# Between two stages of a fused attention and Fourier-mixing kernel: roots and foldings swapped, transposes pinned, copies and memsets moved to another engine

## The chip, the cores and the metric

The kernel runs on one core of a Trainium2 chip. The metric is the device time of one execution in microseconds, as a median over executions. Engines are named as in the profile: PE is TensorE (PEld its weight loads), DVE is VectorE, ACT is ScalarE, POOL is GpSimd, SP is the engine that starts most of the DMAs.

## What is computed

The reference has two parts, one after the other. The first is attention with "talking heads": 8 batches, 12 heads, 448 positions, 64 columns per head. The scores of all heads are mixed by a 12 x 12 matrix before the softmax, and the probabilities are mixed by another one after it. The second is an FNet block on the result, seen as 448 x 768 per batch: the real part of a two-dimensional Fourier transform is added, the rows are normalised, and a feed-forward layer of width 3072 follows. In short:

```python
scores = scale * np.matmul(q, k.transpose(0, 1, 3, 2))
scores = np.einsum('bhij,hg->bgij', scores, w_pre)
attn = softmax(scores)
attn = np.einsum('bhij,hg->bgij', attn, w_post)
x = join_heads(attn @ v)
u = x + np.real(fft2(x))
un = (u - mean(u)) / np.sqrt(var(u) + 1e-06)
out = u + np.maximum(un @ w_ch1, 0.0) @ w_ch2
```

The two weight matrices of the feed-forward layer come as 64-bit floats, and the kernel converts them itself, on DVE, in small pieces dealt out between its other work.

## The kernel before

**Two stages.** `mix_phase` does the attention and the Fourier part. It runs over 192 steps (`TOT`, 24 for each batch, `GS`), with an offset for work that is issued ahead, and up to step 197. A step T takes a slab of mixed scores: the products q k (L443) into `Sb`, a DMA regrouping (L459) into `Kr`, the first mixing (L469), the maximum (L477 on DVE), the exponential (L485 on ACT), the reciprocal (L493 and L494 on DVE), the scaling (L496 on POOL), the second mixing (L506), and a transpose on DVE into `Pv` (L517). Six steps make a group, four groups a batch. For each group, three products with v follow (`emit_av`, L533, 56 matmuls each for pr = 0, 1, 2), whose results ACT copies into `XT` (L324). Columns of `XT` that no row fills are set to zero by POOL (L555). Then PE transposes `XT` into `X` (`emit_x`, L566, six transposes in two halves of three).

**Foldings.** The Fourier transform uses symmetry: after every second group of a batch, `fold` puts eight short POOL steps into the list `folds` (sums and differences of rows and columns: L587, L592, L601, L602), and after the fourth group four more (L608), which make `xf`. The loop takes at most two steps from the list in each of its own steps. For the last batch the first eight are listed at step 188 and so are taken in steps 189 to 192; the last twelve are listed in step 197, after the loop's last look at the list, and are issued by `fold_rest`. From `xf` PE makes `z` (`emit_z`, L631) and from `z` the transform (`emit_s2`, L647), which DVE adds to `X` (L658, L660) and which is then stored to DRAM. The last batch's share of this is carried over as `parts` into the second stage and issued between its products.

**The second stage.** `ffn_phase` works on 7 tiles of 512 rows (`NTB`) and 6 column blocks of weights (`NC`). It uses a seven-product scheme for each pair of blocks: `first` (L946) and `second` (L1002), each in the order `ORDER = (0, 4, 5, 1, 6, 2, 3)`. Before the first product, tile 0 needs: `stats` (L892 and L893 on DVE, four rows of tiles x = 0 to 3), `power` (the roots: L897 to L900 on POOL, which make one over the standard deviation), `norm` (L908 on ACT, `un`, two buffers), `turn` (six transposes per x in two halves y of three, L917 on PE into `psQ`, two buffers; a copy of each half into `ub`, L919 on ACT), `total` (four differences, L925 on DVE, and behind the last seven stores to DRAM, L929 on SP), and `load_w2` (seven loads of weights of the second product, L877 on SP). `un` of x = 2 and 3 needs the buffers of x = 0 and 1. Tiles 1 to 6 are normalised between the products of the tile before them.

**What sets the order.** Inside a `manual_schedule` block, the engines that it names keep the order in which the code issues their instructions. Work of other engines, and how two such blocks lie against one another, is placed by a planner, which reckons when each instruction's inputs will be there and takes the earlier one in the code where several are ready. The mixing loop names PE, DVE, ACT and POOL; the statistics and roots name PE, DVE and POOL; the rest of the second stage names PE and DVE. So ACT's order in the second stage, and SP's throughout, are the planner's.

```python
with tc.manual_schedule(engines={ET.PE, ET.DVE, ET.Pool}):
    for x in range(NT2):
        stats(0, x)
    power(0)
    fold_rest()
with tc.manual_schedule(engines={ET.PE, ET.DVE}):
    for x in range(NT2):
        norm(0, x)
        turn(0, x)
    for n in range(4):
        total(0, n)
    for i in ORDER:
        load_w2(0, i)
```

Of the kernel before, what the change touches and what calls it, by code (L numbers as in the profile page):

```python
# [16 lines left out]
P = 128  # L17
# [30 lines left out]
TOT = B * GS  # L48
# [5 lines left out]
MG = 4  # L54
# [39 lines left out]
NK = DM // 2 // P  # L94
# [190 lines left out]
def mix_phase(ctx, tc, rest, ident, q, k, v, w_pre, w_post, u_scr, u_rev, wts):  # L285
# [6 lines left out]
    nc = tc.nc  # L292
# [28 lines left out]
    pend, folds, later = [], [], []  # L321
# [200 lines left out]
    def emit_av(g, pr):  # L522

        st = batches[g["b"]]
        Pv = g["Pv"]
        rp = _row(Pv)
        nu = GT * 4
        pss = [ms_tile() for _ in range(2)]
        for jb in range(C7):
            for x in range(2):  # L530
                for y in range(2):
                    i = 2 * pr + x
                    nc.tensor.matmul(  # L533
                        pss[y][64 * x:64 * x + 64, :nu * R],
                        st["v", pr][64 * y:64 * y + 64, x, jb * D:(jb + 1) * D],
                        _ap(Pv, 64 * y * rp + 32 * jb + R * i,
                            [[rp, 64], [HS, nu], [1, R]]),
                        start=(jb == 0), stop=(jb == C7 - 1))
        if pr == 0:
            g["XT"] = pxt.tile([P, 6, XW], F32, name="XT", tag="XT")  # L540
        XT = g["XT"]
        rx = _row(XT)
        first, sg, none = PLACE[g["gi"]]

        def done(y):
            rs = _row(pss[y])
            for e in range(2):

                o = MG + first + sg * NB * e
                dst = _ap(XT, (3 * y + pr) * XW + o, [[rx, P], [sg * RS, R], [sg, RS]])  # L550
                src = _ap(pss[y], 60 * e, [[rs, P], [1, R], [R, RS]])
                copy(ENG["AV"][y], dst, src)
            if y == 1 and pr == 2:
                for o in none:
                    nc.gpsimd.memset(XT[:, :, MG + o:MG + o + 1], 0.0)  # L555
        return [lambda y=y: done(y) for y in range(2)]

    def emit_x(g):
# [190 lines left out]
    with tc.manual_schedule(engines={ET.PE, ET.DVE, ET.Activation, ET.Pool}):  # L749
        while s <= TOT - GS + AT_X[-1]:  # L750
            old = len(later)
            n = take("none", s)
            if 0 <= s + LM < TOT:
                emit_premix(s + LM)
            flush()
            if 0 <= s < TOT:
                emit_postmix(s)
            if 0 <= s + LM < TOT:
                emit_max(s + LM)
                emit_exp(s + LM)  # L760
            take("AV", s)
            if 0 <= s < TOT:
                emit_turn(s)
            if s >= 4:
                wts.deal(1)
            take("QK", s)
            if 0 <= s + LG < TOT:
                if any(e[2] is not None and e[2] <= (s + LG) // BS for e in pend):
                    flush()
                emit_gather(s + LG)  # L770
            if 0 <= s + LM < TOT:
                emit_scale(s + LM)
            for _ in range(old):
                later.pop(0)()
            for _ in range(min(len(folds), 1 if n and s > 3 else 2)):
                folds.pop(0)()
            take("full", s)
            s += 1
        flush()
        wts.deal(1000)  # L780
# [26 lines left out]
ORDER = (0, 4, 5, 1, 6, 2, 3)  # L807
# [5 lines left out]
def ffn_phase(ctx, tc, rest, ident, u_scr, u_rev, wts, ub_scr, out, fold_rest,  # L813
# [61 lines left out]
    def load_w2(c, i):  # L875
        w2[i] = pw2.tile([P, FM, DH], F32, name="w2t", tag="w2t")
        nc.sync.dma_start(out=w2[i][:, :, :], in_=wts.w2[c][i])  # L877
# [33 lines left out]
    def turn(t, x):  # L911
        un = uns.pop(x)
        for y in range(2):
            ps = ps_tile("Q")
            for c in range(NK):
                cc = NK * y + c
                nc.tensor.transpose(ps[:, c * P:(c + 1) * P],  # L917
                                    un[:, cc * P:(cc + 1) * P], ident[:, :])
            nc.scalar.copy(  # L919
                out=ubs[t, UB[y, x // 2]][:, :, (x % 2) * P:(x % 2 + 1) * P],  # L920
                in_=ps[:, :NK * P].rearrange("p (c n) -> p c n", n=P))

    def total(t, n):
        o, a, b = ((4, 6, 0), (5, 2, 4), (6, 2, 6), (3, 1, 5))[n]
# [112 lines left out]
    with tc.manual_schedule(engines={ET.PE, ET.DVE}):  # L1037
        for x in range(NT2):
            norm(0, x)
            turn(0, x)  # L1040
        for n in range(4):
            total(0, n)
        for i in ORDER:
            load_w2(0, i)
        for n in range(NC * NTB):
            c, t = divmod(n, NTB)

            if c + 1 < NC and 0 <= t - (c == 0) < NK + FM:
                wts.add(c + 1, t - (c == 0))
            wts.deal(0)  # L1050
            if c == 0 and t + 2 < NTB:
                load_u(t + 2)
            second(n, first(n))
            wts.deal(1000)
            if n == 0:
                assert not parts
                rest.close()
                pu.append(pool("pu2", side="right"))
                beside.close()
                pps.append(pool("ppy", space=bass.MemoryType.PSUM))  # L1060
# [61 lines left out]
```

## Time and profile before

| what | value |
|---|---|
| median of 4 executions | 2429.3 us (2423.35 to 2432.78) |
| the profiled execution's own time | 2425.4 us |
| its span, first to last instruction | 2423.6 us |
| mean granted TensorE clock | 0.996 |
| TensorE busy in the stretch 820.0 to 843.6 us | 21.88 of 23.6 us |
| in 843.6 to 853.1 | 0.00 of 9.5 us |
| in 853.1 to 863.2 | 9.75 of 10.1 us |
| in 863.2 to 868.2 | 3.15 of 5.0 us |
| in 1100 to 2424 | 1319.1 of 1324 us |

A span is the time from the first to the last instruction of one profiled execution; its own time contains a little more around it. The seam between the two stages lies at about 840 to 868 us. Busy times of different engines overlap, so they are not to be added up. In a line of the timeline stand the start in us, the duration of the merged group, the engine, the line of the code, the operation, what it writes and reads, how many instructions there are, and in brackets how long the engine was idle before it and what ended that.

### The profile page before, as it was taken

To read this page: it belongs to the slowest core of one execution; us is meant where nothing else is said; L and a number is where in the kernel's file an instruction comes from. 1 tells how busy PE (TensorE), PEld (TensorE's weight loads), DVE (VectorE), ACT (ScalarE), POOL (GpSimd) and SP (SyncE) were. 2 spreads that over 40 slices of the span, in tenths; PEclk is the share of its full clock that TensorE was granted. 3 is DMA by queue.
4 is the path that set the end of the run, shared out by engine and by line. 5 is a ranking of instruction groups with operands and counts; after the bars stand their busy time and mean duration, and the time that the engine had idled before them with its cause. 6 is when DMAs were issued, how large, how long until landed. Compare 5 with 4: busy or idle time off the path is not lost.

```text
span 2423.6 us, 48510 instructions
## 1 busy us (share of the span) xinstructions
PE 2379.7 (98%) x18608; PEld 1552.7 (64%) x18608; DVE 1505.6 (62%) x3103; ACT 798.7 (33%) x2059; POOL 780.6 (32%) x1293
## 2 busy tenths in 40 slices
PE   7999999999999889999999999999999999999999
PEld 2445454544554477777777777777777777777776
DVE  3777778788787747785567356635665457533333
ACT  4777667666666542322101111111111110110110
POOL 3687877868675531221111011101110011000000
PEclk9999999999999999999999999999999999999999
DMA  6555554646554466346444444535443644353331
GB/s 146 177 182 161 178 174 153 199 156 192 166 167 147 157 208 211 128 151 231 148 136 154 143 145 136 156 116 172 142 152 98 199 127 146 121 167 114 118 117 52
DMA packets 168596, 372.10 MB, mean 154 GB/s; under 512 B 36750, under 2 KB 90022, under 8 KB 168366
## 3 DMA queue, kind: packets, MB, share of 16 engines
q1 hardware_dynamic: 129038, 260.22, 33.2%
q0 software_dynamic: 33760, 107.40, 15.3%
q8 instruction: 149, 2.44, 0.4%
q10 hardware_dynamic: 5568, 1.38, 0.3%
q14 instruction: 81, 0.66, 0.1%
HBM read 211.98 MB, written 74.34 MB: 118 GB/s over the span
## 4 chain that ended last, share of the span: by engine, by line
PE 95%; DMA 2%; SPq 1%; DVE 1%; ACT 1%; issue 0%; ACTq 0%; DVEq 0%
PE psP L946 18%; PE psP L1002 18%; PE psR L946 9%; PE psR L1002 9%; PE mx L469 7%; PE po L506 7%; PE ms L443 6%; PE ms L533 6%; PE psQ L1002 5%; PE psQ L946 4%; PE ms L647 2%; PE ms L420 2%; PE ms L631 1%; DMA Kr<-Sb 1%; PE ms L566 1%; PE psQ L917 1%
## 5 line engine op out<-in xcount | busy, mean ns | idle before, releaser
L946 PE MATMUL psP<-ub,w1t 128*128 128x256 f32 x2016 | 462.6, 379 | 0.0
L1002 PE MATMUL psP<-w2t,h 128*128 128x384 f32 x1344 | 461.0, 486 | 0.0
L946 PEld LDWEIGHTS psP<-ub,w1t 128*128 128x128 f32 x2016 | 382.9, 190 | 60.6
L207 POOL DMA_DIRECT2D raw<-in_moe_w_ch_dram x120 | 68.9, 574 | 923.9 <-DVE tmp L251 905.7
L1002 PEld LDWEIGHTS psP<-w2t,h 128*128 128x128 f32 x1344 | 254.5, 190 | 165.8
L496 POOL TENSOR_SCALAR PP<-PP,rcp 128x448 f32<-128x448 f32 x384 | 240.6, 635 | 236.9 <-DVE rcp L494 106.7
L477 DVE TENSOR_REDUCE nmx<-mx 128x1 f32<-128x448 f32 x384 | 222.2, 618 | 128.4 <-PE mx L469 125.8
L485 ACT ACTIVATE PP<-mx,nmx 128x448 f32<-128x448 f32 x384 | 240.1, 630 | 170.6 <-DVE nmx L477 161.8
L951 ACT COPY h<-psP 128x512 f32<-128x512 f32 x42 | 24.6, 585 | 764.4 <-PE psP L946 753.2
L1008 DVE TENSOR_TENSOR u<-u,psP 128x384 f32<-128x384 f32 x336 | 183.5, 552 | 141.3 <-PE psP L1002 139.1
L946 PE MATMUL psR<-ub,w1t 128*128 128x256 f32 x1008 | 231.3, 379 | 0.0
L1002 PE MATMUL psR<-w2t,h 128*128 128x384 f32 x672 | 230.5, 486 | 0.0
L469 PE MATMUL mx<-Kr,kw 60*64 60x448 f32 x1536 | 222.3, 553 | 7.0 <-DMA Kr<-Sb 4.7
L517 DVE STREAM_TRANSPOSE Pv<-po 128x896 f32<-128x896 f32 x192 | 212.8, 1108 | 14.9 <-PE po L506 12.3
L957 DVE TENSOR_TENSOR h<-h,psQ 128x512 f32<-128x512 f32 x42 | 28.9, 687 | 298.8 <-PE psQ L946 298.6
L946 PEld LDWEIGHTS psR<-ub,w1t 128*128 128x128 f32 x1008 | 191.4, 190 | 25.9
L506 PE MATMUL po<-PP,kw 60*32 60x448 f32 x3072 | 189.0, 548 | 1.3 <-DVE rcp L493 1.3
L324 ACT COPY Sb<-ms 124x448 f32<-124x448 f32 x384 | 184.6, 539 | 16.5 <-PE ms L443 7.2
L443 PE MATMUL ms<-kT,qT 64*64 64x448 f32 (+1 forms) x1536 | 189.2, 553 | 0.0
L533 PEld LDWEIGHTS ms<-Pv,vv 64*64 64x64 f32 x5376 | 144.0, 133 | 69.9 <-issue 32.1
L1002 PEld LDWEIGHTS psR<-w2t,h 128*128 128x128 f32 x672 | 127.3, 190 | 87.4
L533 PE MATMUL ms<-Pv,vv 64*64 64x120 f32 x5376 | 167.0, 269 | 0.8 <-issue 0.8
(92 smaller groups left out, 2751.3 us busy)
## 6 DMA issues: line engine op xcount, KB each, us to landing
ub<-ub SPq DMA_DIRECT2D x294, 384.0 KB
Kr<-Sb SPq DMA_DIRECT2D x768, 105.0 KB
raw<-in_moe_w_ch_dram POOLq DMA_DIRECT2D x72, 256.0 KB, 3.5
raw<-in_moe_w_ch_dram POOLq DMA_DIRECT2D x48, 384.0 KB, 3.8
w<-wst POOLq DMA_DIRECT2D x126, 128.0 KB, 3.1
w<-wst POOLq DMA_DIRECT2D x84, 192.0 KB, 3.2
w1t<-w SPq DMA_DIRECT2D x42, 384.0 KB
w2t<-w SPq DMA_DIRECT2D x42, 384.0 KB
```

What stands on the lines that cost most here:

```text
L324: (nc.scalar.copy if eng == "a" else nc.vector.tensor_copy)(out=out, in_=in_)
L443: nc.tensor.matmul(pss[x][64 * y:64 * y + r0 + 64 - lo, :S], st["qT", xx][64 * x:64 * x + 64, y, lo:r0 + 64], st["kT", xx][64 * x:64 * x + ...
L469: nc.tensor.matmul(mx[x][64 * z:64 * z + 64, :S], kw1[64 * x:64 * x + KR, :], Kr[64 * x:64 * x + KR, z, :], start=True, stop=True)
L477: nc.vector.tensor_reduce(nmx[x][:, :], steps[T]["mx"][x][:, :S], axis=AX.X, op=ALU.max, negate=True)
L485: nc.scalar.activation(PP[:, x, :], steps[T]["mx"][x][:, :S], ACTF.Exp, bias=steps[T]["nmx"][x][:, :], accum_out=den[:, x:x + 1])
L496: nc.gpsimd.tensor_scalar(PP[:, x, :], PP[:, x, :], rcp[:, x:x + 1], 1.0, op0=ALU.mult, op1=ALU.mult)
L506: nc.tensor.matmul(po[o:o + 32, z, :S], kw2[64 * z:64 * z + KR, y, :], PP[64 * z:64 * z + KR, :, c * HS:(c + 1) * HS], start=True, stop=True)
L517: nc.vector.transpose(g["Pv"][:, T % GT, :].rearrange("p (z s) -> p z s", z=2), steps[T]["po"][:, :, :S])
L533: nc.tensor.matmul(pss[y][64 * x:64 * x + 64, :nu * R], st["v", pr][64 * y:64 * y + 64, x, jb * D:(jb + 1) * D], _ap(Pv, 64 * y * rp + 32 ...
L946: nc.tensor.matmul(p[:, m, :], w1[i][:, kc, m * P:(m + 1) * P], ub[:, kc, :], start=i in OPENS and m == kc == 0, stop=kc == NK - 1, skip_g ...
L1002: nc.tensor.matmul(p, lhs[i][:, kf, x * P:(x + 1) * P], w2[i][:, kf, :], start=i in OPENS and kf == 0, stop=kf == FM - 1, skip_group_check ...
L1008: nc.vector.tensor_tensor(us_, us_, p, op=ALU.add)
```

## The change

The change makes five edits, all but the first of them at the seam:

1. The memsets of `XT` (32 in all) are issued on DVE instead of POOL.
2. From step `TOT - 3` (189) on the mixing loop takes nothing from the list of foldings. What is left in the list is issued by `fold_rest`, which stands behind `power(0)`.
3. The very first transpose of `turn` (tile 0, x = 0, y = 0, c = 0) is tied to stay behind the PE instruction issued just before it in the code, which is the last transpose of the mixing loop. The tie is one of order in the queue.
4. For tile 0, the copies of the second half of each x (y = 1) are made by DVE, those of the first half by ACT as before.
5. The loads of the second product's first weights are issued before the differences and the stores behind them, not after.

```diff
@@ emit_av @@
             if y == 1 and pr == 2:
                 for o in none:
-                    nc.gpsimd.memset(XT[:, :, MG + o:MG + o + 1], 0.0)
+                    nc.vector.memset(XT[:, :, MG + o:MG + o + 1], 0.0)
@@ mix_phase, the loop @@
-            for _ in range(min(len(folds), 1 if n and s > 3 else 2)):
-                folds.pop(0)()
+
+            if s < TOT - 3:
+                for _ in range(min(len(folds), 1 if n and s > 3 else 2)):
+                    folds.pop(0)()
@@ turn @@
-                nc.tensor.transpose(ps[:, c * P:(c + 1) * P],
-                                    un[:, cc * P:(cc + 1) * P], ident[:, :])
-            nc.scalar.copy(
-                out=ubs[t, UB[y, x // 2]][:, :, (x % 2) * P:(x % 2 + 1) * P],
-                in_=ps[:, :NK * P].rearrange("p (c n) -> p c n", n=P))
+                tr = nc.tensor.transpose(ps[:, c * P:(c + 1) * P],
+                                         un[:, cc * P:(cc + 1) * P], ident[:, :])
+                if t == x == y == c == 0:
+
+                    tc.keep_in_program_order(tr)
+
+            copy = nc.vector.tensor_copy if t == 0 and y else nc.scalar.copy
+            copy(out=ubs[t, UB[y, x // 2]][:, :, (x % 2) * P:(x % 2 + 1) * P],
+                 in_=ps[:, :NK * P].rearrange("p (c n) -> p c n", n=P))
@@ ffn_phase @@
             norm(0, x)
             turn(0, x)
+        for i in ORDER:
+            load_w2(0, i)
         for n in range(4):
             total(0, n)
-        for i in ORDER:
-            load_w2(0, i)
```

## The prediction

> **What bounds the kernel now.** I read the page first, then the waits of TensorE, then the order of time around the one long wait, engine by engine.
>
> ```profile
> PE 2379.7 (98%) x18608; PEld 1552.7 (64%) x18608; DVE 1505.6 (62%) x3103; ACT 798.7 (33%) x2059; POOL 780.6 (32%) x1293
> ...
> PE psQ L917 <- ACT un L908: 10.3, 2, 9.5
> PE ms L420 <- DMA rawq<-in_q_dram: 7.2, 3, 6.2
> PE ms L420 <- DMA rawk<-in_k_dram: 6.0, 1, 6.0
> PE mx L469 <- DMA Kr<-Sb: 4.7, 5, 1.6
> ```
>
> TensorE is busy for 2379.7 of 2423.6 us, so about 44 us is all that any reordering can win, and the longest single wait is 9.5 us: the first transposes of the feed-forward stage (L917) waiting for the first normalised rows (L908). The timeline of each engine around it:
>
> ```profile
> 838.61 1.25 POOL L496 TENSOR_SCALAR PP<-PP,rcp 128x448 f32<-128x448 f32 x2 [3.79 <-DVE rcp L494]
> 840.02 1.03 POOL L670 DMA_INDIRECT v<-X,rows  x1 [0.16 <-issue]
> 841.07 1.97 POOL L587 TENSOR_TENSOR xs<-X 113x384 f32<-113x384 f32 x2
> ...
> 849.71 0.18 POOL L602 COPY xq<-xs 113x1 f32<-113x1 f32 x1
> 849.99 0.25 POOL L897 TENSOR_SCALAR mv<-mv 128x4 f32<-128x4 f32 x1
> ...
> 842.40 0.21 DVE L893 BATCH_NORM_AGGREGATE mv<-st 128x2 f32<-128x12 f32 x1
> ...
> 841.48 0.80 ACT L324 COPY XT<-ms 128x60 f32<-128x60 f32 x4 [3.57 <-PE po L506]
> 852.02 1.95 ACT L908 ACTIVATE un<-u,mv 128x768 f32<-128x768 f32 x2 [9.75 <-POOL mv L900]
> 853.88 0.78 ACT L324 COPY XT<-ms 128x60 f32<-128x60 f32 x4
> ...
> 843.09 0.47 PE L566 MATMUL ms<-ident,XT 128*113 128x128 f32 x2
> 853.11 0.91 PE L917 MATMUL psQ<-ident,un 128*128 128x128 f32 x3 [9.54 <-ACT un L908]
> 854.36 1.20 PE L566 MATMUL ms<-ident,XT 128*113 128x128 f32 x4 [0.34 <-ACT XT L324]
> 855.48 5.89 PE L533 MATMUL ms<-Pv,vv 64*64 64x120 f32 x168
> ```
>
> Read: start, duration, engine, line. POOL has eight folding steps in its queue before the roots (L897 to L900), though the statistics that the roots need are complete at 842.61. ScalarE's queue holds the third product's copies (XT, 853.88) behind two normalisations, though their input has been there since 843.2. TensorE's queue holds 4 transposes L566, 168 products L533, 8 L647 and 6 L566 behind the three early L917. Two queues, then, must be put right, not one.
>
> ```profile
> 844.48:847.89 3.41, 0.00 (x0) 1.00 0.97 262
> 847.89:851.31 3.42, 0.00 (x0) 0.50 0.98 340
> 851.31:854.72 3.41, 1.27 (x5) 0.50 1.01 392
> 854.72:858.13 3.41, 3.41 (x56) 0.50 0.32 109
> 28.69:32.11 3.42, 1.73 (x9) 1.00 0.24 93
> ```
>
> These are stretches of TensorE (length, busy time, granted clock, DMA share, GB/s). After an empty stretch the clock is 0.50 until 858.13, so the first products after the wait run slow. The last row, early in the kernel, was only half busy, and the clock fell at its end too.
>
> **What the Trainium skill says.** "Perfetto Trace Analysis", section on the TensorE instruction: ScalarE, VectorE and GpSimd take their instructions strictly in order. The trace agrees: the ready XT copies wait from 843.2 to 853.88 behind L908. "TensorE: Matmul & The Clock Gate", "What's actually happening": an idle window of about 3.4 us halves the clock and a busy one restores it; the rows above agree (3.41 us stretches), and the row at 28.69 shows a half-idle one doing the same. "SBUF — State Buffer", "Who interferes with whom": a VectorE instruction with at most one SBUF input does not contend with GpSimd, one with two does. So copies out of PSUM on VectorE should not slow the foldings; that the sums L925 do is seen here: four take 6.10 us beside the foldings, against 1.04 us each on average.
>
> **The change, part by part.**
>
> *Roots ahead of the foldings.* Steps TOT-3 to TOT no longer fold; the eight steps (12 POOL instructions, no DMA, 841.07 to 849.89, 8.8 us) are issued by fold_rest after power(0). POOL is free at 841.05, the statistics end at 842.61, the four roots' instructions take 2.0 us (849.99 to 851.99): the roots end at 844.7, and the first L908 starts at 844.75 instead of 852.02, 7.27 us earlier. The foldings then run 844.7 to 853.5. The second pair's twelve steps wait for the last X (below), as now, so the second Fourier part is not delayed by the swap.
>
> *What is late next.* The planner, not a hand-written order, places ScalarE's L908. It already placed them ahead of the third product's copies, so in its reckoning they were ready sooner; roots without foldings make them sooner still. I take it that they stay ahead. Then the XT copies keep their distance to L908: 853.88 becomes 846.61, and the third L566 goes from 854.36 to 847.09. TensorE is still idle from 843.56 to 847.09. The second product's copies (841.48) may now also fall behind L908; that delays the transposes by 0.7 us more. The softmax cannot: the last statistics stand on VectorE behind the last reciprocal L494, which needs it.
>
> *Transposes pinned behind the mixing's last products.* The first L917 now follows all of L566, L533 and L647 (the other 23 follow by the hand-written order). Warm, 56 products took 1.64 us (838.85 to 840.49), 34 per us; the 168 took 5.82 us, of which 3.17 warm (108), so the slow 2.65 us did 60, 23 per us. After: the idle gap leaves its clock stretch about a quarter busy, so I take half clock from 847.89 to 851.31. L533 starts at 847.7: 6 warm, 78 slow, 84 warm in 2.46 us, end 853.8. From L533's end to the first L917 it is 2.06 us (861.30 to 863.36), hence 855.85. If the second copies also fell behind, 856.35.
>
> *24 transposes instead of 21, copies shared.* Now the 21 take 863.36 to 868.26, 4.9 us, on one copying engine. After, ScalarE still has four copies at 0.44 and two L908 at 1.0 (3.8 us), VectorE four. VectorE's copy of this shape is not in the trace: kT's, 512 columns out of PSUM, takes 0.67 us, so 0.50 for 384 at best; by qT's strided 1.09 us 0.82 at worst; I take 0.5, the destination being rows of 128. VectorE is held by four L658/L660 until 1.6 us after the first L917 (862.90 to 864.85 now). Following two psQ buffers: first half copied at +1.3, L908 for row 2 +1.3 to +2.3, its copy of row 1 +2.7, row 2's transposes +2.75, the last L908 to +3.85, row 3's +4.3 and +4.7, first product L946 at +5.1. Bounds: 24 transposes at 0.14 plus a copy, 3.9; today's pace for all 24, 5.6. So 855.85 + 5.1 = 860.95 against 868.26: 7.3 us gained, 6.8 in the other order. I take 7.1.
>
> *load_w2 before the sums.* Seven SP starts of 384 KB (875.12 to 878.71 now) move past the seven stores L929 (864.89 to 875.03). DMA share is 0.32 and 0.04 in the stretches from 854.7 to 861.6, and 2.7 MB at the 321 GB/s seen need 8.4 us; second products begin some 23 us after the first L946. If the buffers come free only with the last L533, SP is held to about 854 and behind it stand only L929, due after 861, and the next u loads. Nothing either way; the cover is those 23 us.
>
> *Memsets to VectorE.* 32 of 0.11 us, 3.5 us of VectorE work in a stage where TensorE waited for VectorE 3.0 us in all. POOL's memset waited for L566 once in 32 (3.6 us, the last). Behind it on VectorE stand the next L477 and L517. I take nothing; bounds: 1 us gained, 3.5 us lost.
>
> *After the seam.* w1t lands at 852.96 (chain of waits), before 860.95. The first z product (L631) comes 11.7 us after L946, at 872.6; its xf is ready 13.4 us after the second pair's folding starts (863.79 to 877.16 now), so at about 869.6: 3 us spare, as now 2.8. From 869 to the end TensorE is never held for more than 0.3 us, so the gain is kept.
>
> *Sum.* Span 2423.6 - 7.1 = 2416.5; the profiled execution's own time 2425.4 becomes 2418.3. That execution lies 3.9 below the median 2429.3, from which the same gain gives **2422.2**, 0.29% less. A measurement of this kernel can tell about 0.3% (7.3 us) from no change, so the forecast stands on that line.
>
> **Rivals.**
> 1. *The planner puts the third copies ahead of L908.* Then no gap and no slow clock: L533 from 844.2, 4.94 us, first L917 at 851.2, L946 at 856.3, z at 868.0 with xf at 866.9. Gain 12.0: 2417.3. For it: on the chip the copies are ready first. Against: today's order.
> 2. *The gap is too short for the clock to fall.* L533 ends at 852.6, gain 8.4 (7.8): 2421.1. For it: no stretch is empty. Against: the half-busy one at 28.69.
> 3. *The foldings become the bound.* If POOL's twenty steps, with weight loads (L207, 0.57 us each) between them and contention, come 3 us and more later than worked out, L631 waits and later parts too: with 8 us late 5 are lost, about 2427.
> 4. *Slower: memsets in VectorE's queue.* If each holds L477 or L517 while it waits for the transposes of the group before, all 32 cost TensorE. From 0.22 us each the gain is gone; from 0.45 us it is slower by over 0.3%; at 0.5 us, 16 us lost: 2438. Against: POOL's memset waited once in 32.
>
> **How the numbers follow.** Forecast 0.62, its own range 2419.5 to 2425: nearly half of it past the line (0.28 faster, 0.34 same). Rival 1 0.12, faster. Rival 2 0.10 (0.08 faster, 0.02 same). Rival 3 0.08 (0.07 same, 0.01 slower). Rival 4 0.08 (0.01 same, 0.07 slower). Together faster 0.48, same 0.44, slower 0.08. The range runs from just under rival 1 to just over rival 3: 2416.5 to 2427.5.
>
> **What would show it.** L897 within 0.2 us of the last L893, and the first L587 of that stretch behind L900; L908 near 844.8 with XT copies behind it (behind rival 1: ahead of it); the gap before the third L566 3.5 to 4 us; granted clock 0.50 for one stretch; first L917 behind the last L566 near 856; L946 near 861; L919's copies half on VectorE at about 0.5 us; no wait of L631 for xf; L555 on VectorE without idle time. Wrong if TensorE waits for VectorE in the mixing by more than a few us in total, or L631 or L946 waits for a fold or a weight.

## The result, and the profile after

The changed kernel took 2423.6 us as the median of 41 executions (2413.99 to 2433.08); the kernel before took 2428.67 us in the same comparison. The ratio is 0.9972, with a 95% interval of 0.9965 to 0.998: 0.28% less time. In a second comparison (`change_again`, below) it was 0.9969 (0.9958 to 0.998). The profiled execution took 2418.73 us with a span of 2417.0; before's had 2425.42 and 2423.6. So the span became 6.6 us shorter, where 7.1 was forecast.

The change adds some lines, so the line numbers of the second stage move: the roots L897 to L900 are now L899 to L902, the statistics L892 and L893 are L894 and L895, the normalisation L908 is L910, the transposes L917 are L919, their copies L919 are L926, the sums L925 are L931, the stores L929 are L935, the first product L946 is L952, the second L1002 is L1008. The lines of the mixing keep theirs. The experiments below have the lines of the changed kernel.

First the page's line of busy times, and then the waits of TensorE after the change (engine, what it waited in and for, total us, times, longest):

```profile
PE 2378.9 (98%) x18608; PEld 1551.8 (64%) x18608; DVE 1506.9 (62%) x3139; ACT 797.9 (33%) x2055; POOL 778.5 (32%) x1261
```

```profile
PE ms L420 <- DMA rawq<-in_q_dram: 6.2, 2, 5.8
...
PE mx L469 <- DMA Kr<-Sb: 5.5, 5, 2.2
PE ms L566 <- ACT XT L324: 4.3, 1, 4.3
```

TensorE's busy time is 0.8 us less and the span 6.6, so it is mostly idle time that went: 43.9 us before, 38.1 now. The rest is busy time: fewer products run at half clock. The prediction's limit of about 44 us for any reordering counted idle time alone. The wait of 9.5 us for the normalised rows is gone from the list. In its place stands one of 4.3 us, of another instruction for another engine's work: the third product's transposes (L566) for ScalarE's copies of `XT`. The load `rawq` and the regrouping DMAs (`Kr`) are within about 1 us of what they were.

The timeline of the seam, engine by engine (start, duration, engine, line). Two lines of the kernel before come first, the last second mixing and the first product of the second stage:

```profile
840.49 1.00 PE L506 MATMUL po<-PP,kw 60*32 60x448 f32 x16
...
868.26 2.76 PE L946 MATMUL psP<-ub,w1t 128*128 128x256 f32 x12
```

And after the change:

```profile
843.46 0.25 POOL L899 TENSOR_SCALAR mv<-mv 128x4 f32<-128x4 f32 x1 [2.47 <-DVE mv L895]
...
845.22 0.24 POOL L902 TENSOR_SCALAR mv<-mv 128x4 f32<-128x4 f32 x1
845.43 1.95 POOL L587 TENSOR_TENSOR xs<-X 113x384 f32<-113x384 f32 x2
...
842.10 1.02 DVE L894 BATCH_NORM_STATS2 st<-u 128x6 f32<-128x384 f32 x2 [0.48 <-DMA u<-u]
843.16 0.21 DVE L895 BATCH_NORM_AGGREGATE mv<-st 128x2 f32<-128x12 f32 x1
...
845.50 1.95 ACT L910 ACTIVATE un<-u,mv 128x768 f32<-128x768 f32 x2 [3.31 <-POOL mv L902]
847.35 0.78 ACT L324 COPY XT<-ms 128x60 f32<-128x60 f32 x4
...
840.43 1.02 PE L506 MATMUL po<-PP,kw 60*32 60x448 f32 x16
...
843.04 0.47 PE L566 MATMUL ms<-ident,XT 128*113 128x128 f32 x2
847.82 1.20 PE L566 MATMUL ms<-ident,XT 128*113 128x128 f32 x4 [4.31 <-ACT XT L324]
848.95 5.63 PE L533 MATMUL ms<-Pv,vv 64*64 64x120 f32 x168
...
856.57 0.82 PE L919 MATMUL psQ<-ident,un 128*128 128x128 f32 x6
...
861.37 2.75 PE L952 MATMUL psP<-ub,w1t 128*128 128x256 f32 x12
```

GpSimd now waits 2.47 us for the statistics, where before it had eight foldings in front of the roots; the foldings (L587) follow directly. ScalarE starts the normalisations at 845.50, not 852.02. Its next work is still the copy of `XT`, whose input had been there since TensorE's 56 products ended at 843.10: it waits 4.3 us in the queue, and the transposes at 847.82 with it. The first product L952 starts at 861.37, not 868.26, which is 6.9 us earlier.

TensorE's stretches there (length, busy time, granted clock, DMA share, GB/s):

```profile
844.21:847.62 3.41, 0.00 (x0) 1.00 0.77 226
847.62:851.03 3.41, 3.21 (x48) 0.50 0.97 319
851.03:854.44 3.41, 3.41 (x132) 1.00 0.96 351
```

One empty stretch was followed by one at half clock, where 847.89 to 851.31 was forecast. Before there were three at half clock. The prediction had taken the stretch before it as about a quarter busy; it was empty.

### The profile page after: what moved, and what is told of

It reads as the page before. It is cut to its first block, busy times and chain, and to the rows that moved or that the text cites. A ratio compares the mean times of both kernels' runs of the same rounds, so it can differ in the third digit from the quotient of the medians.

```text
span 2417.0 us, 48496 instructions
## 1 busy us (share of the span) xinstructions
PE 2378.9 (98%) x18608; PEld 1551.8 (64%) x18608; DVE 1506.9 (62%) x3139; ACT 797.9 (33%) x2055; POOL 778.5 (32%) x1261
## 3 DMA queue, kind: packets, MB, share of 16 engines
q8 instruction: 149, 2.44, 0.4%
## 4 chain that ended last, share of the span: by engine, by line
PE 96%; DMA 2%; SPq 1%; DVE 1%; ACT 0%; issue 0%; ACTq 0%; DVEq 0%
PE psP L952 18%; PE psP L1008 18%; PE psR L952 9%; PE psR L1008 9%; PE mx L469 7%; PE po L506 7%; PE ms L443 6%; PE ms L533 6%; PE psQ L1008 5%; PE psQ L952 5%; PE ms L647 2%; PE ms L420 2%; PE ms L631 1%; PE ms L566 1%; DMA Kr<-Sb 1%; PE psQ L919 1%
## 5 line engine op out<-in xcount | busy, mean ns | idle before, releaser
L952 PE MATMUL psP<-ub,w1t 128*128 128x256 f32 x2016 | 462.5, 379 | 0.0
L1008 PE MATMUL psP<-w2t,h 128*128 128x384 f32 x1344 | 461.0, 486 | 0.0
L952 PEld LDWEIGHTS psP<-ub,w1t 128*128 128x128 f32 x2016 | 382.9, 190 | 60.6
L1008 PEld LDWEIGHTS psP<-w2t,h 128*128 128x128 f32 x1344 | 254.5, 190 | 165.8
L952 PE MATMUL psR<-ub,w1t 128*128 128x256 f32 x1008 | 231.3, 379 | 0.0
L1008 PE MATMUL psR<-w2t,h 128*128 128x384 f32 x672 | 230.5, 486 | 0.0
L952 PEld LDWEIGHTS psR<-ub,w1t 128*128 128x128 f32 x1008 | 191.5, 190 | 25.9
L506 PE MATMUL po<-PP,kw 60*32 60x448 f32 x3072 | 188.7, 548 | 2.0 <-DVE rcp L493 1.2
L533 PEld LDWEIGHTS ms<-Pv,vv 64*64 64x64 f32 x5376 | 143.6, 133 | 69.8 <-issue 34.3
L1008 PEld LDWEIGHTS psR<-w2t,h 128*128 128x128 f32 x672 | 127.2, 190 | 87.4
L533 PE MATMUL ms<-Pv,vv 64*64 64x120 f32 x5376 | 166.8, 268 | 0.5 <-issue 0.4
```

The source lines that it names most:

```text
L506: nc.tensor.matmul(po[o:o + 32, z, :S], kw2[64 * z:64 * z + KR, y, :], PP[64 * z:64 * z + KR, :, c * HS:(c + 1) * HS], start=True, stop=True)
L533: nc.tensor.matmul(pss[y][64 * x:64 * x + 64, :nu * R], st["v", pr][64 * y:64 * y + 64, x, jb * D:(jb + 1) * D], _ap(Pv, 64 * y * rp + 32 ...
L952: nc.tensor.matmul(p[:, m, :], w1[i][:, kc, m * P:(m + 1) * P], ub[:, kc, :], start=i in OPENS and m == kc == 0, stop=kc == NK - 1, skip_g ...
L1008: nc.tensor.matmul(p, lhs[i][:, kf, x * P:(x + 1) * P], w2[i][:, kf, :], start=i in OPENS and kf == 0, stop=kf == FM - 1, skip_group_check ...
```

## The experiments

Two measures are used beside the ratio. The *seam* is the time from the start of the last second mixing (L506) to the start of the first L952. The *rest* is from that same L506 to the end of the span. They are needed because the mixing ends at another moment in each execution: the last L506 started between 839.05 and 846.71 us in these profiles, whatever the kernel, and a single span moves with it.

| kernel | seam, us | idle before the third L566, us | 168 products L533, us | rest, us | ratio to before |
|---|---|---|---|---|---|
| before | 27.77 | 9.54 and 0.34 | 5.89 | 1583.1 | 1 |
| the change | 20.94 | 4.31 | 5.63 | 1576.6 | 0.9972 |
| change_again | 21.68 | 3.69 | 7.03 | 1577.3 | 0.9969 |
| no_roots | 28.73 | 10.81 | 6.97 | 1584.3 | 0.9999 |
| roots_only | 20.65 | 2.44 and 0.70 | 5.69 | 1576.1 | 0.9983 |
| no_pin | 21.81 | 2.54 and 0.71 | 6.99 | 1577.4 | 0.9969 |
| pool_memset | 22.32 | 4.71 | 6.64 | 1577.9 | 0.9976 |
| w2_late | 20.51 | 3.74 | 6.27 | 1575.9 | 0.9965 |
| act_copies | 20.93 | 3.81 | 5.67 | 1576.3 | one run |
| filler | 20.27 | filled, 1.03 left | 4.66 and 0.42 | 1575.8 | one run |
| xt_first | 15.80 | 0.15 | 5.17 | 1573.3 | 0.9955 |
| xt_first_again | 15.59 | 0.16 | 4.94 | 1573.0 | 0.9961 |
| xt_best | 13.82 | 0.17 | 5.24 | 1572.6 | 0.9957 |

Where two numbers stand in the third column, three early transposes L919 (L917 before) lie between the two gaps.

Differences of about 1 us between the seams of single profiles say little, because two things that the edits are not aimed at move them. One is when the last statistics end after that L506: 2.94 us in the change, 3.30 in pool_memset, and 2.1 to 2.7 in the other kernels of the table. The other is how many stretches at half clock follow the gap: one in the change, roots_only, w2_late and act_copies, two in change_again, no_pin and pool_memset.

### Which edit brings the gain

`no_roots` is the change with the eight foldings back ahead of the roots:

```diff
-            if s < TOT - 3:
+            if True:
```

> The changed kernel with the eight foldings back in steps 189 to 192, so ahead of the roots on POOL; the pin, the shared copies and the rest stay. Theory (the roots' time is what counts, and it reaches TensorE through ScalarE's queue, in which the third XT copies stand behind the two normalisations): roots end near 852.0 again, the third L566 starts at 854.2 to 854.6, the first L952 at 867.5 to 868.3 (861.4 with the change, 868.3 before), span 2423 to 2424, ratio to the kernel before 0.999 to 1.000. Rival (the pin makes the gain, because 9 us of products no longer queue behind the first transposes): the products run from 843.6, and the first L952 is at 858 to 862.

Measured: 2428.37 us, ratio 0.9999 (0.9989 to 1.001). Its timeline:

```profile
854.04 1.94 ACT L910 ACTIVATE un<-u,mv 128x768 f32<-128x768 f32 x2 [10.64 <-POOL mv L902]
855.89 0.78 ACT L324 COPY XT<-ms 128x60 f32<-128x60 f32 x4
...
856.37 1.20 PE L566 MATMUL ms<-ident,XT 128*113 128x128 f32 x4 [10.81 <-ACT XT L324]
```

With the transposes pinned behind the mixing, TensorE waits as long as before, now 10.81 us in L566. All four other edits together show no gain without the swap. The seam is 1.0 us longer than before's, with the 168 products 1.1 us longer.

`roots_only` is the kernel before with edit 2 alone; written against the change:

```diff
-                    nc.vector.memset(XT[:, :, MG + o:MG + o + 1], 0.0)
+                    nc.gpsimd.memset(XT[:, :, MG + o:MG + o + 1], 0.0)
...
-                    tc.keep_in_program_order(tr)
+                    pass
...
-            copy = nc.vector.tensor_copy if t == 0 and y else nc.scalar.copy
+            copy = nc.scalar.copy
...
-        for i in ORDER:
-            load_w2(0, i)
         for n in range(4):
             total(0, n)
+        for i in ORDER:
+            load_w2(0, i)
```

> The kernel before with the second edit alone: no foldings from step 189 on, so the roots come ahead of them; no pin, copies on ScalarE, memsets on POOL, load_w2 behind the sums. The seam is counted from the start of the last L506 to the first L952: 27.8 us before, 20.9 with the change. Theory (this edit is the gain, the others add little at the seam): 20.8 to 21.9 us, ratio to the kernel before 0.9965 to 0.998. Rival (the edits work only together): 23.5 us and more, ratio 0.9985 and up.

Measured: 2423.38 us, ratio 0.9983 (0.9974 to 0.9992), seam 20.65, rest 1576.1.

```profile
841.95 1.03 PE L506 MATMUL po<-PP,kw 60*32 60x448 f32 x16
...
847.49 0.55 PE L919 MATMUL psQ<-ident,un 128*128 128x128 f32 x3 [2.44 <-ACT un L910]
848.74 1.19 PE L566 MATMUL ms<-ident,XT 128*113 128x128 f32 x4 [0.70 <-ACT XT L324]
...
862.60 2.76 PE L952 MATMUL psP<-ub,w1t 128*128 128x256 f32 x12
```

In both profile measures this is the whole gain of the change. Its statistics ended 0.6 us sooner after the last L506 than in the change's profile, so at equal statistics about 0.3 us would be left for the other edits (an estimate from these two profiles). The seam is just under the theory's range, while the ratio lies between the theory's and the rival's. The interval of the ratio overlaps with the change's two (0.9965 to 0.998, 0.9958 to 0.998), but its middle is 0.11 to 0.14% behind; some 3 us from the other four edits, outside the seam, are not excluded by it. No profile here shows where that would be.

### The pin

`no_pin` takes the tie of the first transpose away:

```diff
-                    tc.keep_in_program_order(tr)
+                    pass
```

> The changed kernel without the tie of order: three L919 stand again between the second and the third L566. Theory (TensorE waits at that place for the XT copies anyway, and these stand behind both normalisations): the three L919 start near 846.6 inside the wait, the third L566 at 847.7 to 848.0, the first L952 at 860.9 to 861.7, so no more than 0.5 us from the change. Rival (without the pin the products wait behind the transposes, which is what the pin was to cure): third L566 at 849 or later, first L952 at 863 or later, half of the gain gone.

Measured: 2420.17 us, ratio 0.9969 (0.996 to 0.9979), the same as with the pin. In this profile the last L506 started at 846.30, some 6 us later than in the change's, so the absolute times in the expectation are to be read with that shift.

```profile
848.88 0.47 PE L566 MATMUL ms<-ident,XT 128*113 128x128 f32 x2
851.89 0.55 PE L919 MATMUL psQ<-ident,un 128*128 128x128 f32 x3 [2.54 <-ACT un L910]
853.15 1.20 PE L566 MATMUL ms<-ident,XT 128*113 128x128 f32 x4 [0.71 <-ACT XT L324]
```

Without the pin three L919 run inside the wait. The L566 behind them does not wait for them: it waits for the same `XT` copies, which end later anyway. From the two L566 ahead of the gap to the next four it is 4.27 us here, and 4.78 and 4.17 us in the two profiles of the pinned kernel. The pin moves three transposes out of an idle gap into a busy stretch and releases nothing. The seam of 21.81 us is 0.9 longer than in the change's profile, more than the 0.5 us allowed for, but within 0.2 us of change_again's, which also had two stretches at half clock (6.99 and 7.03 us for the 168 products).

### Memsets, weight loads, copies

`pool_memset` has edit 1 undone:

```diff
-                    nc.vector.memset(XT[:, :, MG + o:MG + o + 1], 0.0)
+                    nc.gpsimd.memset(XT[:, :, MG + o:MG + o + 1], 0.0)
```

> The changed kernel with the 32 memsets back on POOL. Theory (neither engine is what the mixing waits for): seam 20.4 to 21.6 us as with the change, mixing the same, ratio to the kernel before 0.9963 to 0.998. Rival A (the memsets on VectorE hold up the mixing): this kernel faster than the change by 2 us or more, 0.996 and below. Rival B (on POOL they hold up the roots or foldings): 0.9985 and up.

Measured: 2422.56 us, ratio 0.9976 (0.9965 to 0.9988), not to be told from the change. Its seam is 1.4 us longer than in the change's profile, outside the range expected. About 1.0 us of that is the 168 products, with two stretches at half clock instead of one; the other 0.4 us are late statistics, which waited for their rows.

```profile
845.94 1.02 DVE L894 BATCH_NORM_STATS2 st<-u 128x6 f32<-128x384 f32 x2 [1.26 <-DMA u<-u]
```

That wait was 0.48 us in the change, 0.21 in change_again, 0.26 in w2_late. The end of the statistics starts the chain of roots, normalisation and copies: from there to the normalisation it is 2.13 us in this kernel, the change and change_again. Beside change_again the statistics end 1.03 us later here, and the four L566 start 1.02 us later. No memset shows in either part.

`w2_late` has edit 5 undone, the seven weight loads behind the sums again:

```diff
-        for i in ORDER:
-            load_w2(0, i)
         for n in range(4):
             total(0, n)
+        for i in ORDER:
+            load_w2(0, i)
```

> The change with the seven weight loads (load_w2) put back behind the sums in SP's queue, all else as changed. My theory (the move is worth nothing either way, the second products begin some 20 us after the first L952): ratio to before 0.996 to 0.9985 as the change, seam (start of the last L506 to the first L952) 20 to 22.5 us depending on the clock in it, and the seven loads start behind the seven stores, near 869 us on the run's own axis, without any wait of TensorE for them of over 0.5 us. Rival (the early loads take DMA share from the rows u that the statistics wait for, or from the stores L935): then the last statistics no longer wait for u (idle before them under 0.1 us where the change has 0.48) and the seam is 0.5 us or more below 20.9. Second rival (the loads are needed early): second products (L1008) wait for w2t by over 1 us.

Measured: 2420.14 us, ratio 0.9965 (0.9952 to 0.9978), seam 20.51. SyncE's queue in this kernel:

```profile
849.01 4.26 SPq L875 DMA_DIRECT2D w1t<-w  x7
861.14 9.30 SPq L935 DMA_DIRECT2D ub<-ub  x7
870.53 3.41 SPq L879 DMA_DIRECT2D w2t<-w  x7
```

The loads start at 870.53, in the change at 849.99, and TensorE never waits for them in either. The move shows no gain and no loss, and the statistics wait for their rows in both (0.26 us here).

`act_copies` has edit 4 undone, all copies of the transposes on ScalarE:

```diff
-            copy = nc.vector.tensor_copy if t == 0 and y else nc.scalar.copy
+            copy = nc.scalar.copy
```

> The changed kernel with all eight copies L926 of tile 0 on ScalarE. Theory (ScalarE, with two normalisations between, becomes the bound of the transposes): from the first L919 to the first L952 5.6 to 6.1 us instead of 4.8, and the seam longer by as much. Rival (the copies' engine doesn't count, since the buffers are the bound): 4.7 to 5.0 us.

Measured in a single execution: 2417.07 us. Of the 24 transposes the first and the last six, and the product behind them:

```profile
854.70 0.82 PE L919 MATMUL psQ<-ident,un 128*128 128x128 f32 x6
...
859.21 0.93 PE L919 MATMUL psQ<-ident,un 128*128 128x128 f32 x6 [0.75 <-ACT ub L926]
859.98 2.76 PE L952 MATMUL psP<-ub,w1t 128*128 128x256 f32 x12
```

From the first L919 to the first L952 it is 5.28 us, with two copying engines 4.80. So sharing buys 0.48 us: the direction was right, the size about half of what was expected. The whole seam is no longer than the change's (20.93 against 20.94), because here the statistics ended 0.5 us sooner. The sharing pays for the pin: 24 transposes behind the mixing on two engines take 4.80 us, the 21 of roots_only on one take 4.89 (857.71 to 862.60). Together edits 3 and 4 come to about 0.1 us there.

### The gap that is left

`filler` asks what the half clock in the gap costs. It puts 26 transposes of the identity matrix between the second and the third L566; they are computed into a free buffer and never read.

```diff
+    def busy_pe():
+        t = pmx.tile([P, 512], F32, name="mx", tag="mx0")
+        for _ in range(26):
+            nc.tensor.transpose(t[:, :P], ident[:, :], ident[:, :])
...
-            for i in range(3):
+            for i in (j for j in range(3) if not (g is groups[-2] and u == 0 and j == 2 and busy_pe())):
```

> The changed kernel with 26 transposes of the identity into a free PSUM bank between the second and the third L566 of the last group but one; nothing reads them. They keep TensorE busy for most of the 4.3 us wait. Theory (the clock fell because that stretch was mostly idle): granted clock stays at 1.00, the 168 L533 take 4.9 to 5.1 us instead of 5.56, the third L566 still starts near 847.8, and the first L952 is 0.5 to 0.9 us earlier than with the change, at 860.5 to 860.9. Rival (L533 is slow there for another reason, DMA traffic or PSUM buffers): still 5.5 us and more at full clock.

Measured in a single execution: 2419.73 us, seam 20.27; the clock stayed at 1.00.

```profile
849.01 0.72 PE L566 MATMUL ms<-ident,XT 128*113 128x128 f32 x4 [1.03 <-ACT XT L324]
849.65 4.66 PE L533 MATMUL ms<-Pv,vv 64*64 64x120 f32 x164
855.16 0.42 PE L533 MATMUL ms<-Pv,vv 64*64 64x120 f32 x4 [0.84 <-issue]
```

The four L566 take 0.72 us, not 1.20, and the 168 products about 5.0 us without the break before the last four, not 5.63. That break of 0.84 us, put down to no wait that the profile shows, takes back most of it; its cause is open. From the four L566 to the first L952 it is 13.35 us, against 13.55 in the change: the seam is 0.7 us shorter mainly because the statistics ended 0.5 us sooner. The half clock of the change's profile is thus worth some 1.1 us (0.48 + 0.63). In change_again, where two stretches ran at half clock, the 168 products took 7.03 us, 2 us above the 5.0.

`xt_first` tests rival 1, the order in which ScalarE's `XT` copies come ahead of the normalisations. The handles of the copies into `X` are kept (the helper of line 324 is made to return its copy, which is left out below). The first two normalisations of tile 0 are tied to be placed behind the `X` copies of the last group but one, and so behind its `XT` copies, on which these depend:

```diff
-            evs.append(lambda u=u, ps=ps: copy(ENG["X"][u], X[:, u * DH:(u + 1) * DH],
-                                               ps[:PN, :DH]))
+            evs.append(lambda u=u, ps=ps: setattr(wts, f"x{g['b']}{g['gi']}", copy(
+                ENG["X"][u], X[:, u * DH:(u + 1) * DH], ps[:PN, :DH]).ins))
...
-            norm(0, x)
+            with tc.issue_after(wts.x72) if x < 2 else ExitStack(): norm(0, x)
```

> The changed kernel with the first two normalisations of tile 0 tied behind the two X copies of the last group but one, so that the third XT copies and these X copies stand ahead of them on ScalarE. Theory (the 4.3 us before the third L566 are this queue and nothing else): XT copies at 843.2, third L566 at 843.7 with no wait over 0.5 us, granted clock 1.00 throughout, the 168 L533 take 5 us plus at most 1 us of waiting for PSUM buffers, first L919 near 852.0, first L952 near 856.8, then L631 late by about 1 us because xf comes at about 869.4; span about 2413, ratio to the kernel before 0.9950 to 0.9965. Rival (what sets the first L952 is the normalisation itself, or the foldings): first L952 at 860 or later, or L631 held for 4 us or more, so that the time is that of the change, 0.997.

Measured: 2417.77 us, ratio 0.9955 (0.994 to 0.997), seam 15.80.

```profile
844.55 0.80 ACT L324 COPY XT<-ms 128x60 f32<-128x60 f32 x4 [1.81 <-PE ms L533]
...
846.45 1.95 ACT L910 ACTIVATE un<-u,mv 128x768 f32<-128x768 f32 x2
...
845.06 0.72 PE L566 MATMUL ms<-ident,XT 128*113 128x128 f32 x4 [0.15 <-ACT XT L324]
845.70 5.17 PE L533 MATMUL ms<-Pv,vv 64*64 64x120 f32 x168
...
870.43 0.82 PE L631 MATMUL ms<-ts,xf 112*97 112x112 f32 x6 [0.52 <-POOL xf L608]
```

The normalisations stand behind the copies, and nothing misses them: TensorE has the 168 products to do first, at full clock, and the first transposes that need them start at 852.86. The gap is 0.15 us. The last line shows what is late next: GpSimd's second foldings, which now hold L631 for 0.52 us.

That kernel and the change were then run side by side on one chip, as `xt_first_again` and `change_again` (no further edit).

> The same order as in xt_first (normalisations of the first feed-forward tile behind the XT copies of the last group but one), now beside the change itself on the same chip. Theory (the gap before the third product and its half clock are gone, about 5 us): ratio to before 0.9945 to 0.9965, 4 to 6 us below the change's median of this call; seam 15.5 to 17 us. Rival (the 5 us are taken by POOL's second foldings later, as L631 waits for xf): within 2 us of the change's median.

> The change itself, beside xt_first_again on the same chip. Theory: ratio to before 0.9965 to 0.998; the seam 20 to 22.5 us with a gap of about 4 us before the third L566; if the statistics do not wait for u in this run, L910 starts 3 us or less after the last L895 as worked out and the seam is nearer to 20.3.

Measured: 2417.75 against 2420.54 us, ratios 0.9961 (0.9947 to 0.9975) and 0.9969 (0.9958 to 0.998), so 2.8 us between the medians where 4 to 6 were expected, with intervals that overlap. The seams are 6.1 us apart and the rests 4.3. Of the 1.8 us that are lost behind the seam, 1.2 are the wait for `xf` above (0.52 here too) and one of L647 for a copy of `z` (0.7 us). That copy was not late for want of its input: it stood in ScalarE's queue behind two normalisations of the next tile. These start at 880.19, right behind the end of that tile's roots at 880.15 (the profile names a DMA for this wait), and the roots stand behind the second foldings on GpSimd. It is the order of the first gap once more, one tile later.

`xt_best` adds three things to xt_first: one more loop step of foldings ahead of the roots, the normalisations of x = 2 and 3 on VectorE with four `un` buffers and ahead of all transposes of the tile, and three PSUM buffers for the transposes in turn. Written against xt_first:

```diff
-            if s < TOT - 3:
+            if s < TOT - 2:
...
-    pun = pool("pun", 2)
+    pun = pool("pun", 4)
...
-        nc.scalar.activation(uns[x][:, :], us[t][:, x, :], ACTF.Identity,
-                             bias=mvs[t][:, x, 2:3], scale=mvs[t][:, x, 1:2])
+        (nc.vector.tensor_scalar(uns[x][:, :], us[t][:, x, :], mvs[t][:, x, 1:2], mvs[t][:, x, 2:3], op0=ALU.mult, op1=ALU.add) if t == 0 and x > 1 else nc.scalar.activation(uns[x][:, :], us[t][:, x, :], ACTF.Identity,
+                             bias=mvs[t][:, x, 2:3], scale=mvs[t][:, x, 1:2]))
...
-            ps = ps_tile("Q")
+            ps = ps_tile("QPRQ"[x] if t == 0 else "Q")
...
-            turn(0, x)
+        for x in range(NT2): turn(0, x)
```

> The run with the XT and X copies ahead of the normalisations (xt_first, seam 15.8 us, ratio 0.9955), and three steps more: two foldings of step 189 go back ahead of the roots, into the 2 us in which POOL waits for the statistics; the normalisations of rows x = 2 and 3 of tile 0 are made by VectorE ahead of time (four un buffers); and the transposes of tile 0 use PSUM tiles Q, P, R, Q instead of Q alone. Theory (from the first L919 to the first L952 it is the chain of two psQ buffers, 1.2 us for each pair, that counts): these 4.8 us become 3.6 to 4.0, seam 14.6 to 15.1, L631 still held by xf for 0.3 to 1.2 us; ratio to the kernel before 0.9945 to 0.996. Rival (copies on ScalarE and VectorE are the bound whatever the buffers): 4.6 us and more.

Measured: 2418.59 us, ratio 0.9957 (0.9947 to 0.9967). TensorE in its seam, its waits, and ScalarE somewhat later:

```profile
854.17 0.82 PE L919 MATMUL psQ<-ident,un 128*128 128x128 f32 x6
...
856.82 2.76 PE L952 MATMUL psP<-ub,w1t 128*128 128x256 f32 x12
```

```profile
PE ms L647 <- ACT z L324: 1.5, 1, 1.5
...
PE ms L631 <- POOL xf L608: 1.1, 2, 0.6
```

```profile
875.37 2.86 ACT L910 ACTIVATE un<-u,mv 128x768 f32<-128x768 f32 x3 [3.71 <-POOL mv L902]
...
878.66 0.51 ACT L324 COPY z<-ms 96x450 f32<-96x450 f32 x1
```

The transposes go through without a wait, in 2.65 us, better than the 3.6 to 4.0 expected. Yet TensorE waits 2.6 us in L631 and L647, and the rest is only 0.4 to 0.7 us shorter than xt_first's; by the ratio the two kernels cannot be told apart. The products L631 that this `z` is made from were done at 874.42, but its copy came at 878.66, behind three normalisations of the next tile that had waited for their roots. So GpSimd's queue now holds TensorE twice: through the foldings, which is rival 3's mechanism, and through the roots behind them and ScalarE's order. This is reached only once the seam itself is about 5 us shorter than the change leaves it. A tie of order for this copy was not tried.

## Why the prediction was right

The time forecast was 2422.2 us from a median of 2429.3, a gain of 7.1; the two comparisons gave 5.1 (2428.67 to 2423.6) and 7.6 (2428.16 to 2420.54), the profiled spans 6.6, and the rests 6.5 and 5.8 (1583.1 to 1576.6 and 1577.3). By its own steps:

| step of the prediction | written | measured |
|---|---|---|
| roots end, first normalisation starts | 844.7, 844.75 | 845.46, 845.50 |
| third L566 starts, XT copies still behind L908 (now L910) | 847.09 | 847.82 |
| stretch at half clock | 847.89 to 851.31 | 847.62 to 851.03 |
| from the start of L533 to its end | 847.7 to 853.8: 6.1 | 848.95 to 854.51: 5.56 |
| from L533's end to the first transpose | 2.06 | 2.06 |
| 24 transposes, copies on two engines | 5.1 | 4.80 |
| one VectorE copy of 128 x 384 | 0.5 (0.50 to 0.82) | 0.55 to 0.56 |
| first L946 (now L952) | 860.95 | 861.37 |
| first L631 | 872.6, no wait | 873.04, no wait |

*Roots ahead of the foldings.* Right as the source of the gain at the seam, shown by no_roots (ratio 0.9999) and roots_only (seam 20.65 us). They ended 0.76 us later than written, because the sum took the statistics' end from before's profile, 842.61, and in this one it was 843.37: in part their rows came late (0.48 us idle), a DMA that the prediction did not price. The second thing that it took from before, that the planner keeps the normalisations ahead of the copies, held in every kernel that does not force the other order.

*The clock.* Right in size and nearly in place, but partly by luck. The prediction took the places of the stretches from the profile before, and a quarter-busy stretch as enough for the clock to fall; in this profile the stretch was empty, so that reason was not tested at this place. Where the stretches fall on the gap differs between executions: in three of the seven profiles with the gap open and the roots ahead, two stretches ran at half clock and the products took 6.6 to 7.0 us. The two rates worked out from before, 23 products per us at half clock and 34 at full, give for 848.95 to 851.03 some 48 products and for the other 120 another 3.5 us, hence 5.6; 5.56 were measured. The 0.5 us by which the forecast of this term was too long is the later start, nothing else. Rival 2, a gap too short for the clock to fall, did not occur (its argument was that no stretch is empty, and one was): in every kernel with the gap open L533 took 5.6 us or more, against 4.9 to 5.2 without it. filler shows what it would have given, about 1.1 us if its break of 0.84 us is left out.

*The pin and the copies.* The prediction counted 24 transposes behind the mixing instead of 21 and faster copies, and summed them to 5.1 us against 4.9. That was right within 0.3 us, and by act_copies and roots_only it is two terms that cancel: 24 on one engine take 5.28 us, 21 take 4.89. It also said, from "SBUF — State Buffer", "Who interferes with whom" of the Trainium skill, that copies out of PSUM would not slow the foldings while the sums do. (The page's sentence on one SBUF input holds outside VectorE's two-port modes, a limit that the prediction left out.) The trace agrees: two L587 took 1.96 us at 849.88 with VectorE all but idle, 1.96 us at 857.07 beside its additions and copies out of PSUM, and 2.67 us at 861.54 beside the sums.

*Loads and memsets.* Nothing was taken for both. For the loads w2_late shows nothing lost or gained. For the memsets a bound of 3.5 us lost stood beside it, and the slow rival 4 was built on it. On VectorE they take 0.063 us each (0.108 us on GpSimd before), the waits of TensorE for VectorE in the mixing went from 3.0 to 2.3 us, and pool_memset cannot be told from the change. One sign of the prediction failed here: the memsets were to stand on VectorE without idle time, and VectorE idled before 12 of them, 9.6 us in total. It cost TensorE nothing that these runs can tell, so rival 4 is out.

*Rival 1* did not happen in the change but appears to be the better kernel: its forecast was 2417.3 us and xt_first took 2417.77 and 2417.75. It was to gain 12.0 and gained 10 by the rest (1583.1 to 1573.3 and 1573.0). What it lacks lies behind the seam: it had `xf` 1.1 us ahead of L631, and the trace has L631 waiting 0.52 us for it. The second folding pair was taken to begin with the last `X`; with the seam that short it begins behind the first pair and three weight loads in GpSimd's own queue. The wait for `z` was not in that sum. In the one direct comparison with the change the intervals overlap, so that it is the better kernel rests on the profiles and the medians.

So the forecast was right because its links were, with some luck in the clock and in errors of opposite sign: the released stall, the wait that takes its place and the clock in it were each within 0.8 us. The roots came 0.8 us late, the four L566 took 0.5 longer since the clock had fallen just before them (1.13 us, not 0.6), L533 took 0.5 and the transposes 0.3 less, in sum 0.4 late. The gap itself was 4.31 us, where 3.5 to 4 had been named as the sign. What it treated as fixed, and is not, is the length of the mixing ahead of the seam, which differs by several us from one execution to the next. Between the two profiles of the change it accounts for 3.1 of the 3.8 us of difference; the starts of the last L506 in all 13 profiles span 7.7 us. Whether it explains the spread of 2414 to 2433 us of the change's executions was not tested.

## What to carry to other kernels

When a stall at a seam is released, look at what stands next in the queue of the engine that released it: here ScalarE's ready copies behind two normalisations that nobody needed for 10 us more left a gap of 4 us where one of 9.5 had been, and one tie of order removed nearly all of it (0.15 us left). Then look again: one tile later the same pattern held TensorE, with a copy of `z` in ScalarE's queue behind normalisations that waited for their roots. Pinning the waiting engine's own order does nothing where its next instruction waits for the same engine. Compare such edits from a common event (here the last second mixing) to the end, since the part ahead of it varied by more than the edit gains (7.7 us against some 7).

## What the runs showed of the hardware that was not expected

The same 168 products took from 4.94 to 7.03 us, depending on how the stretches of the clock fell on them. The Trainium skill, "TensorE: Matmul & The Clock Gate", "What's actually happening", says that the window runs freely and that the number of slow products so differs from run to run, and these profiles agree. It says that a busy window restores the clock, and gives no share of busy time for it. In the change a stretch with 3.21 of 3.41 us busy at half clock was followed by full clock (above). In change_again one with 2.75 us was not:

```profile
849.61:853.02 3.41, 2.75 (x36) 0.50 0.90 294
853.02:856.43 3.41, 3.41 (x76) 0.50 0.95 295
856.43:859.84 3.41, 3.41 (x85) 1.00 1.03 406
```

It took another, full stretch at half clock before the clock came back. Yet busy time alone does not decide it. Early in pool_memset and in no_roots, again at half clock:

```profile
34.39:37.80 3.41, 2.80 (x14) 0.50 0.34 131
37.80:41.22 3.42, 3.29 (x23) 1.00 0.32 124
...
32.94:36.35 3.41, 2.91 (x12) 0.50 0.34 126
36.36:39.77 3.41, 3.41 (x18) 0.50 0.37 140
```

In the first two rows 2.80 us busy were followed by full clock, in the last two 2.91 us were not. Nor does the clock fall only after an empty stretch: in the change itself one with 1.63 of 3.41 us busy (28.43 to 31.84) was followed by half clock, in pool_memset one with 2.07 (48.04 to 51.45), while one with 2.61 of 3.40 us (838.50 to 841.90 in xt_first) left the clock full. What else decides is not shown here.
